# Another sequence for the first 310 steps of a hand-ordered long convolution with an MLP

## The chip, the cores and the metric

The kernel runs on one core of one Trainium2 chip. The metric is the device time of one execution in microseconds, the median over runs of the same program. Beside the times there is one profiled execution of the kernel before, with its own time; all durations in this document up to the result are from that execution.

## The reference

Sequence length S is 2048, width D is 512, and everything arrives in bfloat16. The model is a gated long convolution followed by a channel-mixing MLP block:

```
k_shift = sum over 4 taps of shifted k times shift_k        (per channel)
kv      = k_shift * v
y       = irfft(rfft(kv, 4096) * rfft(ssm_k, 4096))[:2048] + kv * ssm_D
h       = q + layernorm(q) * y
x       = layernorm(h)
a       = gelu(layernorm(x) @ w1), its four quarters shifted by -1, +1, -2, +2 rows, @ w2
x1      = x + a
out     = h + x1 + gelu(layernorm(x1) @ w3) @ w4            (w3: 512 x 1792, w4: 1792 x 512)
```

The Fourier transforms are over the sequence, one for each of the 512 channels.

## The kernel before, in words

The sequence is cut into halves s = 0 and 1, and each half into eight blocks b of 128 rows. The transforms are done as matrix products in two steps with an exchange of data between partitions in the middle. Four signals are transformed: F0 and F1, the two halves of the filter, and A0 and A1, the two halves of kv. For each signal:

- S1 (L389): eight groups of products of the input blocks with the table f1 on TensorE, named by signal, b and hp.
- E1 (L257, a copy helper): ScalarE or VectorE copies two PSUM banks at a time to SBUF (1024 columns).
- X (L405): eight transfers SBUF to SBUF that regroup the data, named by signal, g and kl. X (sig, g, kl) needs all the E1 of b = 2g and 2g + 1. "X A0 (1,1)" in the title of the change is the one with g = 1 and kl = 1.
- S2 (L413): four groups of products with the table ftab, one for each kl; S2 for kl needs X (0, kl) and X (1, kl).
- E2: copies of the spectrum to SBUF (L257), or for F1 a sum on VectorE (L425).

Before A0 and A1 come the taps: K (L442) makes shifted k by products with diagonals dg, which are built from the taps on VectorE (L307) or POOL (L299), and KV (L450) on VectorE multiplies by v. Each K needs its k load and diagonal, and each KV the load of its half of v. The row with ssm_D is added to row 0 of the filter ("dr", L294, on POOL), which lets the kv * ssm_D term ride in the convolution; S1 of F0 for b = 0 needs it.

The tables are sines, made early: "ftv" computes integer phases (L341), "fta" takes them modulo 4096 (L343), "ft" is the sine on ScalarE (L344); "ttv", "tta" and "tts" make another table, "f2v", "f2a" and "f2s" a third. Then "glu" (L367) loads the Gelu table on ScalarE, after which A0's E1 follow.

The inverse has the spectrum products P (L474, VectorE), the products I2 (L484), their copies EV, eight transfers XI (L495) for each half, and I1 (L502). H (L616) adds q's part: z_t (step Y, L613 on POOL or VectorE, L611 on ScalarE) holds the normalised q, whose statistics Q (L506) run on VectorE as each q block arrives. Then come the two layer norms, w1 (L699), w2 (L722), w3 (L777) and w4 (L790) with the sum of L792 and a store.

Nothing of the order is left to a scheduler. Every piece of work is added to a plan under a number, with a function that issues it, and the string ORDER lists all 784 steps:

```
for word in ORDER.split():
    t, slots, i = self.t[int(word[:3])], [int(c) for c in word[4:]], 0
    ...
        t["fn"](word[3], t["got"].get("ps", slots))
```

The first three digits of a word are the number of the step, the letter is the engine that does it (S SyncE, P TensorE, V VectorE, A ScalarE, G POOL), and the digits behind are the buffers it takes: PSUM banks, or slots of a pool. Each engine does its own steps in the order of the string; across engines they wait for each other by semaphores. A word that changes its letter moves the work to another engine.

All loads, exchanges and stores are issued by SyncE in the order of its words and use one queue. In the built program they take turns on eight semaphores, so each transfer waits until the eighth before it has landed. A load step is no more than this:

```
def load(name, dst, src, deps=(), size=0):
    add(name, {SP: ...}, lambda e, s: nc.sync.dma_start(dst, src), deps, size=size)
```

Names of loads: Lf (half, b) are filter blocks of 256 KB, Lk (half, c) blocks of k of 260 KB, Lv (half, g) parts of v of 512 KB, Lq (half, g) blocks of q of 256 KB, Lw1 to Lw4 the weights. ftab, the integer phases and the A0 spectrum share memory, as do several other pairs, so some orders are fixed by reuse.

Of the kernel before, what the change touches and what calls it, by code (L numbers as in the profile page):

```python
# [33 lines left out]
052A 015S 049G 094V 073S 097P0 054A 040V 024S 050G 091P1 090V 068S 041A 096V 099P4 070S 092V 048A 072S 100V 107P23 069S 103P67 098V 017S 108A 109P45  # L34
067S 111P01 110V 104A 018S 115P23 116A 105P67 323V 113P45 324V 112A 211P20 106V 114A 117P01 212V 119S 084P6745 118A 326V 071S 085A 086V 081P2301 123S
120S 082A 215P6 329V 020S 327V 083A 078P4523 124S 330V 217P7 125S 080A 216V 121S 079A 075P0123 218V 122S 325V 126S 076A 127P6745 328V 011S 128A 219P01
129V 016S 331G 012S 077A 013S 220V 130P6745 139V01 132A 133P2301 131A 141V23 134A 140P45670 147V45 142P 135A 149V67 143A 148P23011 155V01 150P 144A
145S 221P4 152A 146S 157V23 014S 151A 136P6701 222V 138A 137V 153S 156P23452 319G 158P 154S 332G 163V45 225P0 159A 223P1 165V67 160A 161S 164P67230
162S 226V 166P 224V 175P45 167A 168V 333G 213P0 176A 337G0 169S 183P67 170S 340G1 343V2 185P23 184A 214V 177P45 316S 334G3 186V 187P01 178A 189P67
188V 179P45 190A 181P23 180V 028S 182A 171P67 192S 172P01 196S 338V 173P23 191S 335V 339A 349G0 315S 344V 231P45 336A 346G3 195S 235P67 341V 232A  # L40
355G2 198S 347V 174P10 352G1 026S 236A 350V 194S 237P45 358G 356V 348A 193S 202P6723 345A 353V 197S 359G 342A 203V 239P01 238A 371G 360V 241P67 240A
204V 227P45 242A 372G 229P01 228V 230A 199P2367 247S 364G0 373V 233P45 351A 361G1 200V 234A 374G2 362P00 365P1 384V 354A 377G3 208P2345 244S 363V 366A
243S 201V 385G 375P01 367P1 318S 376A 246S 357A 386V 378P0 369P6 390V1 245S 379A 209V 397G 387A0 250S 382P7 248S 368A 210V 388P02 398G 391P2 249S
380P3 389A 025S 392V 370A 399G 263V01 317S 251P0145 383A 381A 393P2 252A 265V23 395P3 253A 027S 205P6701 400V2 396A 403V3 401P43 394A 267V45 404P5
502P3 405A 206V 402A 506P2 406P5 503V 408P4 507V 504A 269V67 508A 264P67231 407A 266P 558V 409A 268P 207V 270P 559G 498P5 560G 271A 272V 561G0 510P4
564G1 499V 494P0 274S 511V 562P10 565P6 495V 514P7 563A 275V01 566A 254P2345 567P60 277V23 256A 577P0 496A 255V 568A 569P1 578A 279V45 573P6 500A 515V
615G 257P4523 574A 575P0 281V67 570A 259A 571P1 501V 576A 579P7 509V 572A 413V 616G 276P23012 580A 517V 278P 513V 280P 282P 412V 617G 581P6 621G2
287V01 283A 258A 285S 505V 273S 512V 618A3 284A 516V 619P71 260P2345 582V 587G 622P0 262A 261V 584P1 583S 588G 623A 620V 289V23 414V 589G 624P00
291V45 636P6 625A 590G0 416V 634P7 293V67 288P45230 635A 411V 290P 592S 591A1 299V01 292P 637A 593S 294P 286S 301V23 628P0 630P7 303V45 629A 295A
632P6 305V67 631A 626P0 297S 633A 417V 296A 300P45671 410V 302P 627A 298S 415V 304P 306P 418V 641P0 307A 419G 308A 309S 310S 420G 430G3 421A0 638P2  # L50
642V 427A2 424G1 497V 643S 594S2 585V 320V 311P34 639V 312P56 640S 422V 313P70 425V 423A 433G0 428V 314P12 426A 436G1 431V 429A 595P30 445V 439A2
442G3 603P6 434V 432A 446G 605P4 437V 604A 447V 435A 597P5 458V 451G3 596A 607P0 438A 448V2 459G 598A 599P3 470V 471G 449P53 452P7 600A 601P6 450V
453A 460V 472G 440V 608A 454P3 602A 473G0 443V 461A1 456P5 441V 474G2 475S 606A 612P2 463S 444A 476S 462A3 482V 455A 464S 483G 457A 477S0 609P3 484V
485V0 486G1 321V 487S 488S 465S1 522P7 489S2 518P6 480P0 519V 478P1 523V 481A 520A 466P0 524A 468P4 479A 644V 467A 490P5 521V 645G 525V 492P6 491A
646V 469A 610V 534P7 493A 647V2 542P3 648V3 649S 535V 554P1 650S 536A 543V 546P0 537V 544A 322V 538P3 545V 651S3 555V 526P5 539V 556A 530P4 611S 547V
540A 586S 550P3 527V 672G 529V 528A 652P50 531V 654P6 551V 673G 653A 656P7 532V 674V 658P3 553V 676A0 675V1 660P1 657A 552V 677S 659A 678S 662P0 756V
661A 557V 655A 664P7 548A 549V 663A 679S0 533V 665A 666P3 700V 757G 613V 758G 728V 701G 669P2 702V 703V2 704G3 705S 614S 729G 706S 730G 760G1 680P40
670V 707S1 686P5 759V0 681A 731V2 667V 688P4 762S 732V3 541V 682P1 761S 668S 684P0 733S 734S 692P6 685A 763S2 689A 708P70 693A 712P0 687A 735S3 714P6
713A 710P0 720P2 711A 764P30 721A 715A 772P0 709A 716P2 736P40 742P5 737A 717A 748P4 683A 738P2 776P1 774P6 777A 743A 766P7 749A 746P1 775A 768P6 747A
770P1 769A 767A 740P5 773A 744P4 765A 741A 771A 778P3 739A 745A 690P2 779V 780S 691A 694P6 750P7 695V 696S 671S 697P6 718P0 719A 725P5 722P4 726V 698V  # L60
727S 699S 753P5 723V 751V 724S 752S 781P4 754V 755S 782V 783S
"""


# [779 lines left out]
```

## Time and profile before

| what | value |
|---|---|
| median of 3 runs | 214.98 us |
| lowest and highest of them | 213.88 and 215.58 us |
| time of the profiled execution | 213.75 us |
| its span, first to last instruction | 211.8 us |
| busy: TensorE | 197.2 us, 93% of the span |
| busy: VectorE | 143.6 us, 68% |
| busy: ScalarE | 127.4 us, 60% |
| busy: POOL | 70.3 us, 33% |
| mean granted TensorE clock | 0.992 |
| share of the chain that ended last on TensorE | 67% |
| on ScalarE, DMA, VectorE, SyncE's queue | 9%, 9%, 7%, 3% |
| moved by the one DMA queue | 32.55 MB |

The profile's page gives busy times over the whole span, which hides that the stages differ: the transforms of the first half and most loads lie in the first third, the MLP in the rest. The views by stretches and the timeline are therefore of more use here than the sums. "Idle before" in brackets in a timeline row is the time that the engine stood still ahead of that row, with what ended it. SPq rows are the issue of a transfer, not its duration; a transfer lands later.

### The profile page before, as it was taken

How to read it: one execution, taken by the hardware profiler on the slowest of the kernel's cores; microseconds unless marked ns; L12 is line 12 of the kernel's file. 1: busy time of each engine (PE TensorE's matmuls, PEld its weight loads, DVE VectorE, ACT ScalarE, POOL GpSimd, SP SyncE). 2: the span in 40 equal slices, each digit the busy share in tenths (PEclk: the TensorE clock that was granted, in tenths of full speed). 3: DMA queues.
4: the chain of work that ended last, by engine and by line, in shares of the span. 5: the costliest groups of instructions: out<-in, count | busy, mean ns of one | idle time of the engine just before them, and what ended most of it. 6: DMA issues, size and time to landing. Idle time of an engine off the chain costs nothing.

```text
span 211.8 us, 5064 instructions
## 1 busy us (share of the span) xinstructions
PE 197.2 (93%) x1980; PEld 117.8 (56%) x1980; DVE 143.6 (68%) x312; ACT 127.4 (60%) x211; POOL 70.3 (33%) x160
## 2 busy tenths in 40 slices
PE   7978876899788999999999999999999999999992
PEld 5544332343237556746654784665848888645440
DVE  6759988999999999999986973389945000020231
ACT  3769996977998965863582984365711655610100
POOL 7480039900995531623007783022370000000000
PEclk9999997999999999999999999999999999999999
DMA  6999698488878994032236007823246600001021
GB/s 179 316 395 384 223 325 321 122 234 257 299 291 286 329 437 144 3 84 68 75 101 176 26 4 178 120 50 99 51 116 156 128 0 0 3 25 50 25 74 50
DMA packets 30808, 32.85 MB, mean 155 GB/s; under 512 B 20545, under 2 KB 22594, under 8 KB 30530
## 3 DMA queue, kind: packets, MB, share of 16 engines
q1 hardware_dynamic: 30786, 32.55, 50.0%
q8 instruction: 15, 0.25, 0.5%
q14 instruction: 7, 0.06, 0.1%
HBM read 13.14 MB, written 4.46 MB: 83 GB/s over the span
## 4 chain that ended last, share of the span: by engine, by line
PE 67%; ACT 9%; DMA 9%; DVE 7%; SPq 3%; issue 3%; ACTq 0%; DVEq 0%
PE ps L777 22%; PE ps L790 20%; PE ps L699 7%; PE ps L722 6%; PE ps L484 5%; ACT r_a L257 4%; DMA r_v<-in_v_dram 4%; DMA r_a<-r_a 3%; SPq L266 2%; ACT r_vs L257 2%; DVE r_p L474 2%; PE ps L502 2%; DMA r_z<-r_vs 2%; PE ps L389 1%; PE ps L413 1%
## 5 line engine op out<-in xcount | busy, mean ns | idle before, releaser
L777 PEld LDWEIGHTS <-r_k 128*128 128x128 bf16 x448 | 43.6, 98 | 7.5 <-issue 0.8
L792 DVE TENSOR_TENSOR r_v<-ps,r_v 128x512 bf16<-128x512 f32 x16 | 10.8, 687 | 46.6 <-PE ps L790 46.6
L474 DVE TENSOR_TENSOR r_p<-r_a,r_f 128x2048 bf16<-128x2048 bf16 x24 | 29.1, 1246 | 0.6 <-ACT r_a L257 0.4
L777 PE MATMUL ps<-r_dg,r_k 128*128 128x256 bf16 x224 | 25.8, 273 | 0.0
L257 ACT CAST r_a<-ps 128x1024 bf16<-128x1024 f32 x23 | 22.4, 1028 | 3.3 <-PE ps L413 2.9
L613 POOL TENSOR_SCALAR z_t<-r_q,qrs,qnm 128x512 f32<-128x512 bf16 x12 | 13.2, 1108 | 13.0 <-DVE r_v L616 12.3
L781 ACT ACTIVATE r_a<-ps 128x512 bf16<-128x512 f32 x14 | 7.9, 609 | 13.8 <-PE ps L777 13.8
L257 ACT CAST r_vs<-ps 128x1024 bf16<-128x1024 f32 x14 | 13.7, 1019 | 4.1 <-PE ps L484 4.1
L257 ACT CAST r_f<-ps 128x1024 bf16<-128x1024 f32 x14 | 13.4, 1031 | 4.5 <-PE ps L389 4.5
L442 PE MATMUL ps<-r_dg,r_k 128*128 128x256 bf16 (+3 forms) x112 | 15.5, 289 | 0.6 <-ACT r_f L257 0.6
L781 ACT ACTIVATE r_f<-ps 128x512 bf16<-128x512 f32 x14 | 7.8, 606 | 13.6 <-PE ps L777 13.6
L484 PE MATMUL ps<-r_p,ttab 32*64 32x512 bf16 x384 | 14.1, 409 | 0.9 <-ACT r_a L257 0.3
L725 DVE SCALAR_TENSOR_TENSOR r_q<-r_v,hrr,ps 128x512 bf16<-128x512 bf16 x16 | 11.3, 743 | 4.9 <-PE ps L722 4.9
L389 PEld LDWEIGHTS <-f 128*32 128x32 bf16 x256 | 7.1, 101 | 12.8 <-issue 8.3
L442 PEld LDWEIGHTS <-r_k 128*128 128x128 bf16 x112 | 9.4, 98 | 8.5 <-issue 4.3
L699 PEld LDWEIGHTS <-r_fx 128*128 128x128 bf16 x128 | 12.2, 98 | 2.5 <-issue 0.4
L777 PE MATMUL ps<-xtx,r_k 128*128 128x256 bf16 x112 | 13.0, 273 | 0.0
L777 PE MATMUL ps<-xty,r_k 128*128 128x256 bf16 x112 | 12.9, 273 | 0.0
L450 DVE TENSOR_TENSOR r_kv<-ps,r_v 128x512 bf16<-128x512 f32 x16 | 10.4, 682 | 3.5 <-DMA r_v<-in_v_dram 3.4
L790 PE MATMUL ps<-w4s,r_f 128*128 128x512 bf16 x56 | 12.7, 379 | 0.0
L748 POOL TENSOR_TENSOR xrr<-xrr,mhalf 128x2 f32<-128x2 f32 x8 | 6.8, 850 | 17.6 <-DVE xrr L745 17.3
L790 PE MATMUL ps<-w4s,r_v 128*128 128x512 bf16 x56 | 12.6, 380 | 0.0
(181 smaller groups left out, 364.7 us busy)
## 6 DMA issues: line engine op xcount, KB each, us to landing
r_z<-r_vs SPq DMA_DIRECT2D x16, 256.0 KB, 3.6
r_k<-in_kt_dram SPq DMA_DIRECT2D x8, 260.0 KB, 4.9
r_v<-in_v_dram SPq DMA_DIRECT2D x4, 512.0 KB, 7.5
r_q<-in_q_dram SPq DMA_DIRECT2D x8, 256.0 KB, 8.0
r_f<-r_f SPq DMA_DIRECT2D x8, 256.0 KB, 4.8
r_a<-r_a SPq DMA_DIRECT2D x8, 256.0 KB, 4.9
r_f<-r_a SPq DMA_DIRECT2D x8, 256.0 KB, 4.4
r_a<-r_z SPq DMA_DIRECT2D x8, 256.0 KB, 8.4
```

The source lines that it names most:

```text
L257: (act.copy if e in "AM" else on[e].tensor_copy)(o, i)
L442: nc.tensor.matmul(o[:, (d + j0) * P:(d + j1 + 1) * P], lhsT=kT[s][c][:, bb, x:x + P], rhs=diag[:, c, j0:j1 + 1, :].rearrange("p j x -> p ...
L474: on[e].tensor_tensor(out=prs[:, sl[0]:sl[0] + 2, :, :], in0=sp[a][:, kl, :, :, :], in1=gv, op=MUL)
L484: nc.tensor.matmul(ps[64 * t:64 * t + 64, bk[h], :], lhsT=ttab[32 * h:32 * h + 32, 2 * kl + t, 2 if x else xx, :], rhs=prs[32 * h:32 * h + ...
L613: on[e].tensor_scalar(out=z_t[:, sl[0], :], in0=qs, scalar1=qrs[:, i:i + 1], scalar2=qnm[:, i:i + 1], op0=MUL, op1=ADD)
L699: nc.tensor.matmul(ps[:, sl[0], j * 256:(j + 1) * 256], lhsT=w1s[:, k, m * P:(m + 1) * P], rhs=xt[:, k, :], start=(k == 0), stop=(k == DC ...
L722: nc.tensor.matmul(ps[:, sl[0], :], lhsT=h1T[s][:, m, bb, x:x + P], rhs=w2s[:, m, :], start=(m == 0), stop=(m == DC - 1))
L725: vec.scalar_tensor_tensor(out=q_sb[:, s, b, :], in0=h_sb[s][:, b, :], scalar=hrr[:, 4 * s + b // 2, 0, b % 2:b % 2 + 1], in1=ps[:, got((" ...
L777: nc.tensor.matmul(ps[:, sl[0], j * 256:(j + 1) * 256], lhsT=w3s[:, k, fc * P:(fc + 1) * P], rhs=xt[:, k, :], start=(k == 0), stop=(k == D ...
L781: act.activation(gb[:, 2 * fp:2 * fp + 2, :], ps[:, got(("M", s, p, fp))[0], :].rearrange("p (j x) -> p j x", j=2), ACT.Gelu_apprx_tanh)
L790: nc.tensor.matmul(ps[:, sl[0], :], lhsT=gb[:, fc, (b % 2) * P:(b % 2 + 1) * P], rhs=w4s[:, fc, :], start=(fc == 0), stop=(fc == FC - 1))
L792: add(("Z", s, b), {V: 0.61}, lambda e, sl, b=b: vec.tensor_tensor(out=h_sb[s][:, b, :], in0=ps[:, got(("O", s, b))[0], :], in1=h_sb[s][:, ...
```

## The change

Only the string ORDER changes. Words 1 to 310 or so (up to place 339, with small swaps near the end) stand in another sequence; from there to the end all words keep their sequence and engine, and only the numbers of PSUM banks and pool slots are renamed. The first lines of the diff:

```
-004S 029P0 000S 002S 003S 005S 008S 031V 037V 009S 030P 063P23 006S 055P45 001S 057P67 064V 007S 056A 038G 065P01 010S 023S 058A 059P45 045G 019S
-061P23 033V 066A 021S 087P60 039V 095P71 036G 046V 101P0 042V 047A 060A 034G 093P1 032G 062A 043V 051P45 074S 088V 035G 044A 053P23 022S 102V 089P6
...
+004S 029P0 000S 002S 003S 005S 008S 031V 037V 001S 030P 063P23 006S 055P45 009S 057P67 064V 007S 056A 038G 065P01 010S 019S 058A 059P45 045G 033V
+061P23 060A 087P60 036V 039G 062A 095P71 046V 042V 066A 093P4 032G 047A 074S 101P5 043V 015S 034G 022S 044A 051P23 094V 023S 053P01 088V 052A 035G
...
```

By names, engine by engine (the order before, then the new one):

- SyncE, first loads: Lk(0,0) Lk(0,3) Lv(0,0) Lk(0,1) Lf(0,0) Lk(0,2) Lv(0,1) Lq(0,2) Lv(1,0) Lq(0,0) X F0 (1,3) ... becomes Lk(0,0) Lk(0,3) Lf(0,0) Lk(0,1) Lv(0,0) Lk(0,2) Lv(0,1) Lv(1,0) X F0 (1,3) Lk(1,0) Lq(0,1) Lq(0,2) X F0 (1,1) Lq(0,3) Lq(0,0) ...
- SyncE, the A0 exchange: X A0 (0,0), X F0 (1,0), X A0 (1,0), (0,1), Lv(1,1), X A0 (1,1), (1,2), (0,2), (0,3), (1,3), Lf(1,0), Lk(1,1), Lf(1,1) becomes X F0 (1,0), X A0 (0,0), (1,0), (0,1), (1,1), Lv(1,1), X A0 (1,2), (0,2), Lf(1,1), Lf(1,0), Lk(1,1), X A0 (0,3), (1,3).
- SyncE, later: Lw1 and Lw2 change places; Lq(1,1) goes from among the F1 exchanges to behind X A1 (1,3); X A1 (0,3) and (0,2) go ahead of Lw3.
- VectorE and POOL: ftv goes from VectorE to POOL, the diagonal for c = 3 from POOL to VectorE, a small memset (edge0, L573) from POOL to VectorE, and Y (0,3), one z_t, from VectorE to POOL. POOL does dr ahead of the diagonal for c = 1, not behind it.
- VectorE: the gating products KV run in the order (0,3), (0,0), then fta, (0,1), (1,0), (0,2), (1,3), (1,1), (1,2). Before: (0,0), (1,3), (0,3), fta, (0,1), (1,0), (0,2), (1,2), (1,1). Two E1 of F1 change places between VectorE and ScalarE.
- ScalarE: E1 F0 (2,0) and (2,1) go ahead of f2s and of E1 F0 (3,1); some copies of the same kind and three HS (L600) change places.
- TensorE: neighbours change places (K (0,3) and (1,3), K (0,2) and (1,1), five pairs of S1, one I1 and an S1).

More of the change, by code (lines that the diff above doesn't have):

```diff
@@ L36 @@
[L36 to L59, printed above, removed]
@@ new lines @@
+150P 144A 145S 221P4 333G 157V23 152A 146S 337G0 014S 151A 136P0123 222V 343G1 137V 138A 156P45672 153S 340G2 158P 154S 334G3 163V45 225P2 159A 223P3
+160A 165V67 161S 164P01450 162S 226V 166P 224V 175P67 167A 168V 213P2 176A 169S 183P01 214V 170S 185P45 184A 187P67 315S 186V 177P23 188A 189P01 178V
+179P45 190A 181P67 180V 171P01 028S 182A 172P23 338V 192S 231P67 196S 335V 339A 349G0 173P45 316S 344V 336A 346G3 193S 341V 235P01 232A 355G1 195S
+347V 174P32 236A 352G2 191S 350V 237P67 198S 358G 342A 356V 202P0145 197S 348A 353V 194S 345A 359G 204V 239P23 238A 371G 203V 241P45 240A 227P67 242A
@@ new lines @@
+229P23 372G 360V 228V 230A 199P0145 247S 361G0 373V 233P67 351A 364G1 200V 362P20 234A 374G2 365P3 384V 366A 377G3 208P0167 245S 363V 354A 375P31 243S
+201V 385G 367P2 376A 244S 357A 378P3 386V 246S 369P4 379A 390V0 318S 209V 397G 387A1 382P5 248S 370A 250S 388P32 210V 368A 398G 391P4 026S 380P0 389A
+249S 383A 392V 399G 251P2367 263V01 025S 381A 393P1 317S 252A 265V23 027S 395P0 253A 205P4523 396A 400V2 394A 403V3 401P03 267V45 404P1 502P6 405A
+206V 402A 506P7 406P1 503V 408P0 507V 504A 269V67 508A 264P45671 407A 266P 558V 409A 268P 207V 270P 559G 498P1 560G 271A 272V 561G1 510P0 564G0 499V
@@ new lines @@
+494P2 274S 511V 562P30 565P4 495V 514P5 563A 275V01 566A 254P6701 567P40 277V23 256A 577P2 496A 255V 568A 569P3 578A 279V45 573P4 500A 515V 615G
+257P0167 574A 575P2 281V67 570A 259A 571P3 501V 576A 579P5 509V 572A 413V 616G 276P67232 580A 517V 278P 513V 280P 282P 412V 617G 581P4 621G2 287V01
+283A 258A 285S 505V 273S 512V 618A3 284A 516V 619P51 260P6701 582V 587G 622P2 262A 261V 584P3 583S 588G 623A 620V 289V23 414V 589G 624P20 291V45 636P4
+625A 590G1 416V 634P5 293V67 288P01670 635A 411V 290P 592S 591A0 299V01 292P 637A 593S 294P 286S 301V23 628P2 630P5 303V45 629A 295A 632P4 305V67 631A
@@ L62 @@
+731V2 667V 688P0 762S 732V3 541V 682P3 761S 668S 684P2 733S 734S 692P4 685A 763S2 689A 708P50 693A 712P2 687A 735S3 714P4 713A 710P2 720P6 711A 764P70
+721A 715A 772P2 709A 716P6 736P00 742P1 737A 717A 748P0 683A 738P6 776P3 774P4 777A 743A 766P5 749A 746P3 775A 768P4 747A 770P3 769A 767A 740P1 773A
+744P0 765A 741A 771A 778P7 739A 745A 690P6 779V 780S 691A 694P4 750P5 695V 696S 671S 697P4 718P2 719A 725P1 722P0 726V 698V 727S 699S 753P1 723V 751V
+724S 752S 781P0 754V 755S 782V 783S
 """
```

16 lines of the change are left out of this document (12 added, 4 removed).

## The prediction

> **What bounds the kernel now.** I read the page first, then the chain of work that ended last, the busy time by stretches, and the timeline of the first 50 us, where every moved step lies.
>
> ```profile
> span 211.8 us, 5064 instructions
> PE   7978876899788999999999999999999999999992
> DVE  6759988999999999999986973389945000020231
> ...
> ```
>
> Each digit is the busy share of a fortieth of the span (5.3 us) in tenths. TensorE has no gap worth naming from its fourteenth slice (about 69 us) until the end; its loose slices are the first thirteen, where the change lies. VectorE is just as full from its fourth slice to its twentieth.
>
> ```profile
> 10.00:15.00 5.00, 3.83 (x40) 2.23 (x38) 2.79 (x5) 3.40 (x5) 3.77 (x7) 1.00 1.06 416
> 25.00:30.00 5.00, 4.39 (x63) 1.95 (x63) 4.88 (x9) 5.00 (x7) 0.21 (x2) 1.00 0.79 255
> 30.00:35.00 5.00, 2.48 (x41) 0.90 (x40) 3.78 (x4) 3.15 (x4) 4.70 (x11) 0.97 1.00 365
> 35.00:40.00 5.00, 4.68 (x75) 2.00 (x73) 4.63 (x5) 4.76 (x6) 4.81 (x4) 0.69 0.36 128
> 100.00:110.00 10.00, 9.77 (x177) 6.42 (x175) 9.97 (x14) 6.81 (x12) 0.00 (x0) 1.00 0.34 86
> ```
>
> The columns are the stretch, then busy time of PE, weight loads, VectorE, ScalarE and POOL, the granted clock, the DMA share and GB/s. From 30 to 35 us PE works half the time and VectorE three quarters; this is the only slack stretch between 15 us and the end in which both wait. From 100 to 110 us both are full. So whatever the first 45 us save moves the rest forward as a block; whatever they save ahead of a full engine that gets no less work is handed back.
>
> ```profile
> 5.61 8.06 DMA r_v<-in_v_dram
> 13.79 1.29 DVE r_kv L450 x2
> 15.08 0.98 DVE r_a L343
> 16.09 1.15 ACT ftab L344
> 17.26 1.28 ACT L367
> 18.66 2.05 ACT r_a L257 x3
> 24.15 1.03 ACT r_f L257
> 26.56 0.59 SPq L266
> 27.20 5.42 DMA r_a<-r_a
> 32.75 0.67 PE ps L413 x16
> ...
> 35.42 1.99 PE ps L484 x26
> ```
>
> The chain (start, length, what) says it in order: the second half of v lands at 13.67 us, VectorE gates with it, the sine table and the Gelu table follow on ScalarE, which then evacuates from 18.66 us on; SyncE issues the second half of v for the second half-sequence at 26.56 us and only then X A0 (1,1), which lands at 32.62 us, and the second transform of A0 starts at 32.75 us.
>
> **The change part by part.** Part one, the start.
>
> ```profile
> 7.81 1.32 DVE L341 TENSOR_SCALAR r_a<-r_a,sv 128x512 int32<-128x512 int32 x2
> 7.98 0.87 POOL L299 TENSOR_SCALAR_AFFINE_SELECT r_dg<-r_k 128x512 bf16<-128x512 bf16 x1 [1.27 <-DMA r_k<-in_kt_dram]
> 7.16 0.74 DVE L307 TENSOR_SCALAR r_dg<-ident,r_k 128x128 bf16<-128x128 bf16 x4 [1.12 <-DMA r_k<-in_kt_dram]
> 9.53 1.90 ACT L257 CAST r_f<-ps 128x1024 bf16<-128x1024 f32 x2
> 11.12 0.63 POOL L299 TENSOR_SCALAR_AFFINE_SELECT r_dg<-r_k 128x512 bf16<-128x512 bf16 x1 [2.27 <-DMA r_k<-in_kt_dram]
> 11.80 1.14 POOL L294 TENSOR_TENSOR r_fx<-r_fx,r_vs 1x512 bf16<-1x512 bf16 x1
> 12.99 1.05 PE L389 MATMUL ps<-r_fx,f 128*32 128x512 bf16 x16 [1.17 <-POOL r_fx L294]
> 13.79 1.29 DVE L450 TENSOR_TENSOR r_kv<-ps,r_v 128x512 bf16<-128x512 f32 x2 [2.17 <-DMA r_v<-in_v_dram]
> ```
>
> PE waits 1.17 us for the row sum of filter block 0 (L294), which POOL does behind a diagonal (L299) that itself waits 2.27 us for k. In the new order L294 stands ahead of that diagonal and block 0 is loaded two places earlier, ahead of the first half of v and of k block 1. Three transfers change places among themselves, so the last of them still ends near 11.7 us (the diagonal's k landed at 11.1 us, and L294 found block 0 there 0.7 us later): block 0 then lands near 8.7 us and the first half of v near 11.7 us instead of 10.3. POOL has first the two table operations that VectorE did in 1.32 us; on POOL I bound them by 1.3 us and by 4.2 us (two at 2.1 us, a row on z_t below), so L294 ends between 9.9 and 12.1 us. PE reaches its matmuls at 11.82 us: 0.9 to 1.17 us of its wait goes. VectorE takes one diagonal more (0.74 us) while it waited anyway.
>
> The gating is reordered: before, the second product needs the second half of v, and VectorE sat 2.17 us; now four that need only the first half stand in front. From 11.75 us: two products at 0.65 us, the table's AND (L343, 0.98 us on the chain), then six more products end at 18.2 us instead of 19.0. The AND ends at 14.2 us instead of 16.06, and from its end to ScalarE's first A0 evacuation the chain has 2.6 us (18.66 less 16.06), so that could start at 16.8 us. PE, some 1.1 us ahead of before, ends the first A0 product at 17.1 us. ScalarE begins the A0 evacuations at 17.2 us, not 18.66: 1.45 us gained there.
>
> Part two, from there to the exchange; the rows are of the timeline, SPq being the issue queue, and the last one is from the instructions on r_v.
>
> ```profile
> 20.58 1.28 DVE L506 BATCH_NORM_STATS2 qst<-r_q 128x6 f32<-128x512 bf16 x2
> 23.05 0.52 SPq L405 DMA_DIRECT2D r_a<-r_a  x1
> 24.31 2.21 SPq L405 DMA_DIRECT2D r_a<-r_a  x2
> 27.20 3.64 SPq L405 DMA_DIRECT2D r_a<-r_a  x5
> 29.63 1.23 DVE L257 CAST r_a<-ps 128x1024 bf16<-128x1024 f32 x1
> 32.07 0.69 DVE L450 TENSOR_TENSOR r_kv<-ps,r_v 128x512 bf16<-128x512 f32 x1 [1.22 <-DMA r_v<-in_v_dram]
> 32.68 2.35 DVE L474 TENSOR_TENSOR r_p<-r_a,r_f 128x2048 bf16<-128x2048 bf16 x2
> 35.40 5.05 DVE L474 TENSOR_TENSOR r_p<-r_a,r_f 128x2048 bf16<-128x2048 bf16 x4 [0.37 <-ACT r_a L257]
> 35.48 6.36 POOL L613 TENSOR_SCALAR z_t<-r_q,qrs,qnm 128x512 f32<-128x512 bf16 x3
> 46.97 0.54 DVE L613 TENSOR_SCALAR z_t<-r_q,qrs,qnm 128x512 f32<-128x512 bf16 x1
> DMA to landing us min/median/max: 5.4/7.5/8.6
> ```
>
> All of q's first half now queues behind v's first 512 KB of the other half-sequence and behind four other transfers: after the 13.67 us of v's second half stand nine units of 256 KB before the q block that VectorE's statistics need first; at 416 GB/s that is 0.63 us each, so it lands at 19.4 us, 20.5 if an issue stalls (every transfer here waits for the eighth before it). VectorE arrives at 19.4 us. I take 0.35 us of waiting. Behind that statistics row on VectorE stand the A0 evacuation and, behind it, SyncE's first A0 exchange: 22.45 us instead of 23.05. VectorE then does the same list to the cast that began at 29.63 us, plus the edge memset: it now begins near 29.15 us. So of 1.45 us about 0.5 is left: VectorE has hardly a gap in this stretch (4.88 of 5 us between 25 and 30).
>
> Part three, the exchange. Before, SyncE spends 0.6 us on an F0 exchange between the first and second A0 one, then 2.21 us on the next two, then v, then X A0 (1,1) at 27.20 us. Now the F0 one is already gone (it waits only for older transfers) and the order is A0, A0, A0, X A0 (1,1), v. At 0.6 us an issue, with ScalarE's sixth A0 evacuation ready at 23.1 us (17.2 us and the 5.5 us that six took from 18.66 to 24.15, and 0.4 us for a k product of PE in between), (1,1) is issued at 24.3 us and v at 24.9 us; if one issue takes the extra 1.0 us seen at 24.31 us, at 25.3 and 25.9. As many transfers stand ahead of v as before, so 5.4 us from issue to landing (the row's smallest, and that of this transfer, since VectorE got it at 32.0 us) gives 30.3 to 31.3 us; I take 30.9. The transform then waits for VectorE's cast (30.4 us) instead of for (1,1): 2.3 us earlier than 32.75, but it isn't last. Last is v, since VectorE has the k-v product (L450) in front of the spectrum products (L474). L450 ends at 31.6 us and L474 begins then instead of at 32.68: 1.1 us. The 0.37 us wait in the next row goes too, since its casts start 2 us earlier. The sum on VectorE at 40 us: 1.1 + 0.37 = 1.47 us, bounds 0.9 (v at 31.4) and 1.85 (v under VectorE's own 30.3).
>
> Part four, one z_t (0.54 us at 46.97 us) goes from VectorE to POOL. The next cast behind it starts as PE's matmul ends, so nothing is gained there; cover gone, it would be 0.54. POOL's row shows 2.1 us each, so four end near 44 us instead of three near 42; their reader (L616) is further back on VectorE than the z_t at 46.97 us. A rule of the Trainium skill speaks against it: "SBUF — State Buffer", section "SBUF: two separate sides", has VectorE operations with two SBUF inputs and GpSimd operations that read SBUF exclude each other for a whole instruction. By the rows the four products beside z_t took 1.26 us each against 1.18 in the pair before, 0.08 more. By the rule one more z_t could cost VectorE up to its whole own time, and the gain would be less by that.
>
> The weight loads of w1 and w2 change places, a q block goes from before the F1 exchanges to behind the A1 ones, and w3 goes behind two A1 exchanges: all still ahead of their use.
>
> ```profile
> r_k<-in_w_dram SPq DMA_DIRECT2D x1, 1792.0 KB, 9.0
> 82.53 3.39 PEld L777 LDWEIGHTS <-r_k 128*128 128x128 bf16 x32 [0.41 <-DMA r_q<-in_q_dram]
> ```
>
> w3 takes 9.0 us to land and is first read at 82.53 us; SyncE has its issue behind two exchanges more, 1.2 us, and its place in the sequence is still some ten microseconds ahead of that, so 0; without that cover it would be 1.2 us. The last 445 steps keep their order and engines; only bank numbers differ.
>
> The sum: 1.47 us, rounded 1.5. The profiled execution took 213.75 us, 1.95 above its span of 211.8, so 212.25 for one like it; the median shown is 214.98, 1.23 us higher, so I forecast 213.5 us.
>
> **The rivals.**
>
> First, more: with the early transform the gap of PE between 30 and 35 us may go under what drops its clock (0.97 and 0.69 in the two rows; at half speed that is 0.3 and 3.1 us, 3.4 in all). The 1.99 us of L484 on the chain then take 1.0 us, v lands before 30.3 us, and z_t's 0.54 counts: 1.85 us from there, 0.4 us of L484's 1.0 that lies on the chain ahead of VectorE's next product, and 0.54: 2.8 us, 212.2 us. Against it: PE still waits between the products at 1.2 us each. The Trainium skill ("TensorE: Matmul & The Clock Gate", "Part 1: The HAM clock gate") has a free-running window of about 3.4 us that decides on the clock; the trace's half-speed spell fits it, and by that the drop may merely fall somewhere else.
>
> Second, nothing: VectorE's full stretch hands back all. If q lands at 20.5 us, its 0.5 us goes; if v lands at 31.9 us, only the 0.37 us is left, which the next exchange wait can take: 214.7 to 215.0 us. For it: VectorE's 4.88 of 5. In this case the change does what it says (block 0 and (1,1) come earlier) and neither was last.
>
> Third, slower: v, now behind one A0 exchange more in its own queue, lands late, and L450 holds every L474 behind it. The row for r_v goes up to 8.6 us from issue to landing: 24.9 + 8.6 = 33.5 us, L474 begins at 34.2 us instead of 32.68, and with the 0.37 us spared the loss is 1.2 us: 216.2 us. It decides from a landing of 32.4 us on. For it: the same queue also has three new loads behind v, ahead of two exchanges. Against it: the loads that took 8.6 us had the queue full before them; at 25 us the share is 0.79.
>
> **How the numbers follow.** Forecast 0.45, more 0.22, nothing 0.15, slower 0.18. The forecast's own range is 212.9 to 214.3 us (0.9 to 1.85 us, with 0.2 about it). The runs of before spread from 213.9 to 215.6 us, so I let the range reach over the first rival and nearly all of the third: 211.7 to 216.2 us. One per cent, 2.15 us, is about what a measurement of this kernel can tell from no change. Faster by more than that: the first rival and a quarter of the forecast's scatter, 0.34. Slower by more than that needs the third with scatter on top: 0.12. Within: 0.54.
>
> **What would show it.** In the changed profile: PE's matmuls of filter block 0 without the 1.17 us wait; the Gelu table load near 15.6 us; the first A0 exchange at 22.5 us; (1,1) issued before 25.5 us; the first L474 at 31 to 32 us without a wait of 0.37 us behind it; the steady stretch of PE beginning 1.5 us earlier. Wrong if L450 waits for r_v past 32 us, if the statistics wait for r_q more than 1 us, or if L474 begins 1.5 us earlier and the end does not follow.

## The result

| | before | changed |
|---|---|---|
| median, lowest and highest of 20 runs each | 214.24 us, 212.09 to 215.58 | 212.9 us, 211.56 to 214.98 |
| ratio of changed to before | | 0.9931, 95% interval 0.9905 to 0.9957 |
| profiled execution, and its span | 213.75 us, 211.8 | 211.95 us, 209.8 |
| mean granted TensorE clock in it | 0.992 | 1.000 |

The ratio is 1.5 us of 214.24, with an interval from 0.9 to 2.0 us. A second session gave 0.9954 (0.9920 to 0.9988), 1.0 us. The ratios and intervals leave out executions more than 1.5% above the fastest of their kernel: two of the changed kernel's twenty here, up to nine of 35 of the kernel before in the sessions below.

The page of the changed kernel, the same three lines as before:

```profile
span 209.8 us, 5064 instructions
PE   7999775999889999999999999999999999999992
DVE  6997989999999999999968862489935000020231
```

The loose slices are still in the first quarter, the rest is the same wall of nines. By stretches (start and end, busy PE, weight loads, VectorE, ScalarE, POOL, granted clock, DMA share, GB/s):

```profile
10.00:15.00 5.00, 4.94 (x49) 2.96 (x48) 4.93 (x9) 3.85 (x6) 3.10 (x6) 1.00 1.00 382
30.00:35.00 5.00, 2.41 (x64) 0.65 (x59) 4.08 (x5) 4.62 (x6) 4.67 (x6) 1.00 0.96 362
35.00:40.00 5.00, 3.93 (x87) 1.76 (x87) 5.00 (x6) 4.49 (x5) 4.89 (x4) 1.00 0.56 159
```

PE now works 4.94 of the 5 us from 10 to 15 us (3.83 before) and VectorE 4.93 (2.79). From 30 to 35 us PE still works only half the time. From 35 to 40 us the clock is full where it had been 0.69, and PE's work there takes 3.93 us instead of 4.68. The chain of work that ended last, its pieces up to 32 us:

```profile
2.49 3.62 DMA r_k<-in_kt_dram
6.13 3.33 DVE r_dg L307 x8
...
14.36 1.05 ACT ftab L344
15.43 1.28 ACT L367
...
24.17 1.35 SPq L405
...
27.41 3.65 DMA r_q<-in_fx_dram
...
31.53 1.23 DVE r_p L474
```

v's second half no longer opens the chain; the first k block and eight diagonals on VectorE do. The sine table is at 14.36 us instead of 16.09. X A0 (1,1) is issued at 24.17 us, 27.2 before. Just ahead of L474 the chain goes through a filter block issued behind v, which landed at 31.06 us, within 0.3 us of v: two waits end almost together there. The timeline of the same execution:

```profile
8.26 1.14 POOL L294 TENSOR_TENSOR r_fx<-r_fx,r_vs 1x512 bf16<-1x512 bf16 x1
11.44 1.05 PE L389 MATMUL ps<-r_fx,f 128*32 128x512 bf16 x16
16.83 5.57 ACT L257 CAST r_a<-ps 128x1024 bf16<-128x1024 f32 x6
19.84 1.28 DVE L506 BATCH_NORM_STATS2 qst<-r_q 128x6 f32<-128x512 bf16 x2 [1.32 <-DMA r_q<-in_q_dram]
22.31 3.21 SPq L405 DMA_DIRECT2D r_a<-r_a  x4
25.57 0.59 SPq L266 DMA_DIRECT2D r_v<-in_v_dram  x1
28.68 1.21 DVE L257 CAST r_a<-ps 128x1024 bf16<-128x1024 f32 x1
29.76 0.79 PE L413 MATMUL ps<-r_a,ftab 64*32 64x512 bf16 x16
30.92 0.69 DVE L450 TENSOR_TENSOR r_kv<-ps,r_v 128x512 bf16<-128x512 f32 x1 [1.04 <-DMA r_v<-in_v_dram]
31.53 6.90 DVE L474 TENSOR_TENSOR r_p<-r_a,r_f 128x2048 bf16<-128x2048 bf16 x6
```

Block 0's products (PE L389) stand without a wait; the second A0 transform starts at 29.76 us, 32.75 before; v is still what L450 waits for, and all six L474 run without the 0.37 us wait between them.

### The profile page after: what moved, and what is told of

It is laid out like the page before. It is cut to its first block, busy times and chain, and to the rows that moved or that the text cites. A ratio compares the mean times of both kernels' runs of the same rounds, so it can differ in the third digit from the quotient of the medians.

```text
span 209.8 us, 5064 instructions
## 1 busy us (share of the span) xinstructions
PE 196.0 (93%) x1980; PEld 116.6 (56%) x1980; DVE 143.8 (69%) x314; ACT 127.6 (61%) x211; POOL 72.2 (34%) x161
## 4 chain that ended last, share of the span: by engine, by line
PE 64%; DVE 14%; ACT 8%; DMA 6%; SPq 3%; issue 3%; POOL 0%; DVEq 0%; ACTq 0%
PE ps L777 23%; PE ps L790 20%; PE ps L722 6%; PE ps L699 4%; PE ps L484 4%; DVE r_p L474 3%; ACT r_a L257 3%; DMA r_dg<-dhb 2%; DVE r_v L616 2%; PE ps L502 2%; SPq L405 2%; DVE r_f L425 2%; DMA r_q<-in_fx_dram 2%; DMA r_k<-in_kt_dram 2%; DVE r_dg L307 2%
## 5 line engine op out<-in xcount | busy, mean ns | idle before, releaser
L474 DVE TENSOR_TENSOR r_p<-r_a,r_f 128x2048 bf16<-128x2048 bf16 x24 | 28.5, 1225 | 0.2
L613 POOL TENSOR_SCALAR z_t<-r_q,qrs,qnm 128x512 f32<-128x512 bf16 x13 | 15.3, 1186 | 9.9 <-DVE r_v L616 9.2
L442 PE MATMUL ps<-r_dg,r_k 128*128 128x256 bf16 (+3 forms) x112 | 15.5, 288 | 0.9 <-ACT r_f L257 0.8
L484 PE MATMUL ps<-r_p,ttab 32*64 32x512 bf16 x384 | 12.6, 379 | 2.1 <-DVE r_p L474 1.5
L442 PEld LDWEIGHTS <-r_k 128*128 128x128 bf16 x112 | 9.5, 98 | 9.0 <-issue 4.2
L699 PEld LDWEIGHTS <-r_fx 128*128 128x128 bf16 x128 | 12.3, 98 | 3.1 <-issue 0.8
L389 PEld LDWEIGHTS <-f 128*32 128x32 bf16 x256 | 6.2, 96 | 11.9 <-issue 8.2
L790 PE MATMUL ps<-w4s,r_f 128*128 128x512 bf16 x56 | 12.7, 379 | 0.0
L790 PE MATMUL ps<-w4s,r_kv 128*128 128x512 bf16 x56 | 12.4, 379 | 0.0
```

The costliest lines, as they stand in the source:

```text
L442: nc.tensor.matmul(o[:, (d + j0) * P:(d + j1 + 1) * P], lhsT=kT[s][c][:, bb, x:x + P], rhs=diag[:, c, j0:j1 + 1, :].rearrange("p j x -> p ...
L474: on[e].tensor_tensor(out=prs[:, sl[0]:sl[0] + 2, :, :], in0=sp[a][:, kl, :, :, :], in1=gv, op=MUL)
L484: nc.tensor.matmul(ps[64 * t:64 * t + 64, bk[h], :], lhsT=ttab[32 * h:32 * h + 32, 2 * kl + t, 2 if x else xx, :], rhs=prs[32 * h:32 * h + ...
L613: on[e].tensor_scalar(out=z_t[:, sl[0], :], in0=qs, scalar1=qrs[:, i:i + 1], scalar2=qnm[:, i:i + 1], op0=MUL, op1=ADD)
L699: nc.tensor.matmul(ps[:, sl[0], j * 256:(j + 1) * 256], lhsT=w1s[:, k, m * P:(m + 1) * P], rhs=xt[:, k, :], start=(k == 0), stop=(k == DC ...
L790: nc.tensor.matmul(ps[:, sl[0], :], lhsT=gb[:, fc, (b % 2) * P:(b % 2 + 1) * P], rhs=w4s[:, fc, :], start=(fc == 0), stop=(fc == FC - 1))
```

## The experiments

All but the last move one or more words of ORDER, or change the engine of one; the last is the changed kernel as it is. In the first eight kernels the string takes two lines less, so in their rows L448 is L450, L472 is L474, L440 is L442, L387 is L389, L411 is L413, L403 is L405, L292 is L294, L297 is L299 and L504 is L506. The first four ran on one chip, the next four on a second, the last four on a third, each group with runs of the kernel before beside it; a ratio is always to those.

**Filter block 0 ahead of v, alone.**

```
-037V 009S 030P 063P23 006S 055P45 001S 057P67
+037V 001S 009S 030P 063P23 006S 055P45 057P67
```

> The kernel before with one load moved: filter block 0 ahead of the first half of v, nothing else. Theory (only what reaches the first L474 on VectorE counts, and the gating of A0 waits for v's second half): PE's 1.17 us wait on L294 goes or shrinks under 0.5 us, but the AND (L343) still ends at 16.1 us because the second product in VectorE's order needs the second half of v at 13.7 us. ScalarE begins A0's evacuations at 18.4 to 18.7 us, L474 begins at 32.4 to 32.8 us, time within 0.3 us of before. Rival (the named edit gains by itself): PE runs 1.1 us earlier and the end follows, 1.0 to 1.2 us faster than before.

Measured: ratio 0.9992 (0.9960 to 1.0024). The theory on the time held, its reason did not. From the timeline:

```profile
11.05 0.64 POOL L297 TENSOR_SCALAR_AFFINE_SELECT r_dg<-r_k 128x512 bf16<-128x512 bf16 x1 [2.76 <-DMA r_k<-in_kt_dram]
11.65 1.14 POOL L292 TENSOR_TENSOR r_fx<-r_fx,r_vs 1x512 bf16<-1x512 bf16 x1
12.84 1.05 PE L387 MATMUL ps<-r_fx,f 128*32 128x512 bf16 x16 [1.36 <-POOL r_fx L292]
```

PE's wait did not go, it grew from 1.17 to 1.36 us. The row sum stands behind a diagonal on POOL that waits 2.76 us for k, and no earlier load of block 0 moves that.

**The gating order, alone.**

```
-053P23 022S 102V 089P6 ... 054A 040V 024S
+053P23 022S 089P6 ... 054A 040V 102V 024S
```

> The kernel before with one word of VectorE moved: the gating product (1,3), the one that needs v's second half, behind the AND (L343); all loads as before. Theory: the AND ends near 13.3 us instead of 16.06, but PE's wait on L294 is still there, so ScalarE reaches the sine only after its F0 evacuations, near 15.6 us: A0's evacuations begin at 18.2 to 18.5 us instead of 18.66, time 0 to 0.5 us faster than before. Rival (the gating order was the whole gain at the start): A0's evacuations begin at 17.2 us or earlier, time 0.8 us faster or more.

Measured: 1.0013 (0.9974 to 1.0051), no gain; A0's evacuations began at 19.02 us, later than both theories said.

```profile
15.82 3.68 DVE L448 TENSOR_TENSOR r_kv<-ps,r_v 128x512 bf16<-128x512 f32 x6 [1.25 <-PE ps L440]
```

VectorE no longer waits for v but for the k products of PE, which stand behind block 0's.

**Both of these.**

> The kernel before with both: filter block 0 loaded ahead of v's first half and the gating product (1,3) behind the AND; q, v's other half and the exchange in the order of before. Theory: each gate hid the other, so together ScalarE begins A0's evacuations 1.0 to 1.45 us earlier (17.2 to 17.7 us), more than the two single edits added; VectorE is full from there and X A0 (1,1) still behind v, so 0.3 to 0.9 us faster than before. Rival 1: all of the 1.45 us arrives at the end. Rival 2: VectorE hands all back, within 0.2 us of before.

Measured: 1.0032 (0.9998 to 1.0067), rather slower; A0's evacuations at 19.36 us. The theory fell: the two together don't open the gate. The same wait is 1.85 us here:

```profile
16.16 3.08 DVE L448 TENSOR_TENSOR r_kv<-ps,r_v 128x512 bf16<-128x512 f32 x5 [1.85 <-PE ps L440]
```

A third piece was missing, which these kernels left as it was: the row sum's place on POOL.

**X A0 (1,1) ahead of v, alone.**

```
-020S 327V 083A 078P4523 124S 330V
+124S 020S 327V 083A 078P4523 330V
```

> The kernel before with one transfer moved on SyncE: X A0 (1,1) issued ahead of the second 512 KB of v. Theory: the transform of A0 that needs (1,1) begins near 30 to 31 us instead of 32.75, but v is issued about 0.6 us later, so L450 and the first L474 begin 0 to 0.6 us later; the 0.37 us wait among the products goes. Time within 0.4 us of before, either way. Rival (the exchange was the limit, as the title has it): L474 at 40 us is 1 to 2 us earlier and the time 1 to 2 us shorter.

Measured: 0.9984 (0.9951 to 1.0017), as the theory said; L474 began 0.2 us later than before, behind a wait of 1.49 us for v, and its 0.37 us wait was gone.

**The changed kernel with v back ahead of X A0 (1,1).**

```
-124S 083A 215P6 020S
+020S 124S 083A 215P6
```

> The changed kernel with one transfer put back on SyncE: the second 512 KB of v issued ahead of X A0 (1,1), all else as changed. Theory: v is issued 0.6 to 1.3 us earlier and L450 with it, so the first L474 begins 0.3 to 1.0 us earlier than 31.53 us, but the transform that waits for (1,1) is 1 to 2 us later and its products with it; within 0.6 us of the changed kernel. Rival (the exchange's place is the gain): the time goes back by 1 us or more towards before.

Measured: 1.0042 (1.0005 to 1.0079): the whole gain is gone, as the rival had it. Alone the exchange was worth 0.2%, in the changed order about 1%. The two figures compare sessions on different chips. The profiled execution shows a part of why:

```profile
21.39 1.29 DVE L504 BATCH_NORM_STATS2 qst<-r_q 128x6 f32<-128x512 bf16 x2 [1.79 <-DMA r_q<-in_q_dram]
28.34 1.36 PE L440 MATMUL ps<-r_dg,r_k 128*128 128x512 bf16 x7
33.28 6.91 DVE L472 TENSOR_TENSOR r_p<-r_a,r_f 128x2048 bf16<-128x2048 bf16 x6
```

The first L474 comes at 33.28 us, not earlier but later. v didn't hold it: VectorE waited 1.79 us for q, and further on 1.24 us for a group of seven k products of PE, which took 1.36 us (1.03 elsewhere) at a granted clock of 0.66 from 25 to 30 us. The six L472 run without the 0.37 us wait here too, although (1,1) is behind v. How much of the 2 us is the exchange's place and how much the clock of this execution stays open. The loss in time is not a matter of the clock alone: the four executions without a stretch of lower clock are 0.58 us slower than such executions of the kernel before.

**The changed kernel with the q block that is read first in front of the other q blocks.**

```
-022S 044A 051P23 ... 091P6 021S 049G
+021S 022S 044A 051P23 ... 091P6 049G
```

> The changed kernel with one load moved: the block of q that VectorE's statistics (L506) read first goes ahead of the other three. Theory: the 1.32 us wait at 19.8 us is a real loss; without it VectorE's A0 evacuation starts near 20 us and the first A0 exchange is issued at 21.0 to 21.4 us instead of 22.31, v up to 1 us earlier, L474 near 30.6 us; 0.5 to 1.0 us faster than the changed kernel. Rival (v's landing is set by the queue and not by its issue, or VectorE waits for PE instead): the wait moves to another row and the time is within 0.3 us.

Measured: 1.0007 (0.9973 to 1.0041): not faster than the changed kernel, rather 0.5 to 0.8% slower.

```profile
21.77 3.23 SPq L403 DMA_DIRECT2D r_a<-r_a  x4
31.12 0.69 DVE L448 TENSOR_TENSOR r_kv<-ps,r_v 128x512 bf16<-128x512 f32 x1 [1.37 <-DMA r_v<-in_v_dram]
```

The wait for q went, the first A0 exchange was issued 0.54 us earlier and v at 25.04 instead of 25.57 us, and yet v landed at 31.1 us. That fits the rival, that the landing is set by what the queue still has to move more than by the issue; one profile doesn't show it. Ten of its twelve executions had a stretch of lower clock (below); why this order has it so often isn't shown.

**The changed kernel with v ahead of the first A0 exchange.**

```
-119S 326V ... 215P6 020S
+020S 119S 326V ... 215P6
```

> The changed kernel with one load moved: the second 512 KB of v goes ahead of the first A0 exchange. Theory (v's landing is the last wait ahead of L474): v is issued near 20 to 22 us and lands by 28 us, the 1.04 us wait of L450 goes, L474 begins at 30.5 to 30.9 us; 0.5 to 1.0 us faster than the changed kernel. Rival (the exchanges behind it in the queue pay): A0's exchanges land 0.6 to 1.3 us later, the transform takes over as the last wait, and the time is the same or up to 0.7 us slower.

Measured: 0.9918 (0.9884 to 0.9952), 212.08 us median, the lowest of all kernels. Its interval overlaps both of the changed kernel's, so it beats before, and is not shown to beat the changed one.

```profile
21.14 0.60 SPq L264 DMA_DIRECT2D r_v<-in_v_dram  x1
29.02 0.63 PE L411 MATMUL ps<-r_a,ftab 64*32 64x512 bf16 x16 [1.34 <-DMA r_a<-r_a]
29.80 1.23 DVE L255 CAST r_a<-ps 128x1024 bf16<-128x1024 f32 x1 [0.94 <-ACT r_f L255]
31.54 6.90 DVE L472 TENSOR_TENSOR r_p<-r_a,r_f 128x2048 bf16<-128x2048 bf16 x6
```

Theory and rival are both in the trace: v no longer holds L450, and the A0 exchange, now behind v, holds the transform for 1.34 us instead.

**The changed kernel with both, q and v.**

> The changed kernel with both moves: the first q block that the statistics read goes ahead of the others, and v's second 512 KB goes ahead of the first A0 exchange. Theory: the two waits lie one behind the other on VectorE, so both gains add: L474 near 30 us, 1.0 to 1.8 us faster than the changed kernel. Rival (something else, PE's transform or its S1 of F1, is next in line): no more than the better of the two single moves, under 0.8 us.

Measured: 0.9959 (0.9921 to 0.9998), the rival: L474 at 31.55 us, as with v alone, though the first A0 exchange was issued 0.4 us earlier. The transform's wait for the exchange was 1.34 us again.

**The kernel before with the start of the changed one: load, row sum ahead of the diagonal on POOL, gating order.**

```
-009S ... 001S      -034G 093P1 032G      -102V ... 040V
+001S 009S ...      +032G 034G 093P1      +... 040V 102V
```

> The kernel before with the three moves of the start: filter block 0 loaded ahead of v's first half, the row sum (L294) on POOL ahead of the diagonal that waits for k, and the gating product (1,3) behind the AND. All loads of q and v's other half and the exchange as before. Theory (the row sum's place on POOL, not the load, was what PE waited for): PE's wait on L294 goes, the gating no longer waits 1.85 us for PE, ScalarE begins A0's evacuations at 17.2 to 17.8 us instead of 18.66 and L474 follows by 0 to 0.6 us; v and X A0 (1,1) keep their order, so the time is 0.2 to 0.7 us shorter than before. Rival 1 (the start was the whole gain): 1.2 us shorter or more. Rival 2 (with X A0 (1,1) behind v nothing arrives at the end): within 0.2 us.

Measured: 0.9965 (0.9935 to 0.9996), 0.75 us, nearest to the theory. Against the kernel with load and gating alone the one more word, 032G, is worth 0.7% (by ratios from two chips).

```profile
8.42 1.30 POOL L294 TENSOR_TENSOR r_fx<-r_fx,r_vs 1x512 bf16<-1x512 bf16 x1
8.64 1.14 DVE L365 TENSOR_SCALAR r_a<-r_a 128x64 int32<-128x64 int32 x1
11.46 1.18 PE L389 MATMUL ps<-r_fx,f 128*32 128x512 bf16 x16
31.76 2.35 DVE L474 TENSOR_TENSOR r_p<-r_a,r_f 128x2048 bf16<-128x2048 bf16 x2
34.48 5.05 DVE L474 TENSOR_TENSOR r_p<-r_a,r_f 128x2048 bf16<-128x2048 bf16 x4 [0.37 <-ACT r_a L257]
```

PE's wait is gone, the gating still waits 0.67 us for PE, and L474 is 0.92 us earlier with its 0.37 us wait still there. The row sum's move without the other two was not run; it may carry all of this.

**The same with X A0 (1,1) ahead of v.**

```
-020S 327V 083A 078P4523 124S 330V
+124S 020S 327V 083A 078P4523 330V
```

> The kernel before with the three moves of the start and X A0 (1,1) issued ahead of v's second 512 KB; the loads of q, k and the weights, z_t, the diagonals and the tables' engines as before. Theory (start and exchange together are the change, everything else in it is filler): L474 begins at 31.3 to 31.9 us, the time is 1.0 to 1.7 us shorter than before, the same as the changed kernel within 0.4 us. Rival (the q blocks behind v and the other small moves carry part of it): less than half of the changed kernel's gain, under 0.7 us.

Measured: 0.9936 (0.9901 to 0.9970), 1.4 us. These four words bring what the changed kernel brings, within what can be measured; the other moved words are not shown to bring anything. Some of them may cost: the changed kernel with v back ahead of (1,1) has the start too, and yet it was 0.8% slower than the start alone. The q blocks behind v, for which VectorE waited 1.79 us there, are one candidate, but the kernel in which that wait went by another order of q was not faster either; it stays open. The exchange's own part here, 0.3%, lies inside both intervals, and in the profiles L474 begins later with it (32.08 us, the theory had 31.3 to 31.9) than without (31.76). In the timeline the 0.37 us wait is gone:

```profile
32.08 6.90 DVE L474 TENSOR_TENSOR r_p<-r_a,r_f 128x2048 bf16<-128x2048 bf16 x6
```

**The changed kernel with v ahead of the first A0 exchange and ftv back on VectorE.**

```
-036V 039G 062A      -119S 326V ... 215P6 020S
+036V 039V 062A      +020S 119S 326V ... 215P6
```

> The changed kernel with v's second 512 KB ahead of the first A0 exchange and the two table operations ftv (L341) back on VectorE. Theory (VectorE and POOL hinder each other at 6 to 10 us: eight diagonals took 3.3 to 3.6 us beside ftv on POOL, where four took 0.74 alone): diagonals and ftv on VectorE take about 2.8 us together, the AND ends 0.4 to 0.8 us earlier and ScalarE's A0 evacuations with it; but q's first block and the exchange stay where they are, so 0 to 0.5 us faster than with v's move alone, the best time of all kernels near 211.7 us. Rival (POOL needs the port too or VectorE waits for v's first half at 11.7 us): the gain is under 0.1 us, or the loss up to 0.5 us.

Measured: 0.9958 (0.9923 to 0.9992), not better than v's move alone.

```profile
6.15 0.81 DVE L307 TENSOR_SCALAR r_dg<-ident,r_k 128x128 bf16<-128x128 bf16 x4
7.14 0.74 DVE L307 TENSOR_SCALAR r_dg<-ident,r_k 128x128 bf16<-128x128 bf16 x4 [0.18 <-DMA r_k<-in_kt_dram]
7.80 1.83 DVE L341 TENSOR_SCALAR r_a<-r_a,sv 128x512 int32<-128x512 int32 x2
7.91 1.44 POOL L294 TENSOR_TENSOR r_fx<-r_fx,r_vs 1x512 bf16<-1x512 bf16 x1 [1.15 <-DMA r_fx<-in_fx_dram]
29.79 0.62 PE L413 MATMUL ps<-r_a,ftab 64*32 64x512 bf16 x16 [2.22 <-DMA r_a<-r_a]
```

Eight diagonals took 1.55 us instead of 2.84 to 3.61, but L341 now met the row sum and took 1.83 us (1.32 before). The evacuations of A0 began at 17.32 us, 0.3 earlier than with v's move alone; then the exchange landed later still (2.22 us of waiting) and took it all back.

**The changed kernel, profiled once more.**

> The changed kernel itself, profiled a second time. Theory (of the 2.0 us between the two profiled spans about 1 us is the luck of that execution, in which the first k block landed so early that VectorE began its diagonals at 6.13 us without a wait, where every other kernel waited 0.9 to 1.3 us): this time the diagonals begin at 6.9 to 7.3 us, ScalarE's A0 evacuations at 17.6 to 17.9 us and L474 at 31.8 to 32.5 us; the time stays 0.5 to 0.9 per cent under before. Rival (the early k belongs to the change's order of loads): the diagonals begin again at 6.1 to 6.3 us.

Measured: 0.9954 (0.9920 to 0.9988), and a span of 212.0 us where the first profiled execution had 209.8, both at a clock of 0.998 or more.

```profile
span 212.0 us, 5064 instructions
...
5.48 4.46 PE L389 MATMUL ps<-r_fx,f 128*32 128x512 bf16 x40 [0.90 <-DMA r_fx<-in_fx_dram]
6.81 3.61 DVE L307 TENSOR_SCALAR r_dg<-ident,r_k 128x128 bf16<-128x128 bf16 x8 [0.76 <-DMA r_k<-in_kt_dram]
13.46 1.05 PE L389 MATMUL ps<-r_fx,f 128*32 128x512 bf16 x16
18.70 1.93 ACT L257 CAST r_a<-ps 128x1024 bf16<-128x1024 f32 x2
21.78 1.29 DVE L506 BATCH_NORM_STATS2 qst<-r_q 128x6 f32<-128x512 bf16 x2 [1.43 <-DMA r_q<-in_q_dram]
33.26 0.69 DVE L450 TENSOR_TENSOR r_kv<-ps,r_v 128x512 bf16<-128x512 f32 x1 [1.43 <-DMA r_v<-in_v_dram]
33.87 6.90 DVE L474 TENSOR_TENSOR r_p<-r_a,r_f 128x2048 bf16<-128x2048 bf16 x6
```

The rival's early k did not come back here; it did in the kernel with ftv back on VectorE (6.15 us), so two of the seven profiles with this order of loads have it and none of the other seven. Luck fits this best; a part of the order in it isn't excluded. The sizes were missed: ScalarE's A0 evacuations at 18.70 us where 17.6 to 17.9 was expected, L474 at 33.87 where 31.8 to 32.5 was. Another filter block came so late that PE waited 0.90 us at the beginning, and block 0's products stood 2.0 us later than in the first execution. This execution was the slowest of its twelve (214.15 us), the first one the third fastest of its twenty (211.95), so the two profiles show the ends of the scatter and not its middle.

**The three stretches.** From the same timelines: the start of ScalarE's first A0 evacuation; from there to the first L474; from there to the pair of L474 behind the A0 cast that began at 41.03 us in the kernel before; and from that pair to the end. All in us.

| kernel | to A0's evacuation | to first L474 | to the pair | to the end | half-speed clock |
|---|---|---|---|---|---|
| before | 18.66 | 14.02 | 9.68 | 169.4 | 3.4 |
| load alone | 18.07 | 14.62 | 10.32 | 169.7 | 6.8 |
| gating alone | 19.02 | 13.47 | 9.68 | 169.3 | 3.4 |
| load, gating, no row sum | 19.36 | 13.59 | 10.47 | 169.2 | 6.8 |
| exchange alone | 18.59 | 14.29 | 10.00 | 169.3 | 6.8 |
| start alone | 17.77 | 13.99 | 9.68 | 169.3 | 3.4 |
| start and exchange | 18.08 | 14.00 | 10.00 | 169.2 | 6.8 |
| changed, first profile | 16.83 | 14.70 | 8.74 | 169.5 | 0 |
| changed, second profile | 18.70 | 15.17 | 8.74 | 169.4 | 0.8 |
| changed, v back | 17.94 | 15.34 | 8.79 | 169.6 | 3.4, ahead of L474 |
| changed, q first | 17.58 | 14.15 | 10.01 | 169.7 | 6.8 |
| changed, v early | 17.66 | 13.88 | 9.08 | 169.9 | 3.4 |
| changed, q and v | 17.80 | 13.75 | 8.79 | 170.3 | 0, 1.3 near the end |
| changed, v early, ftv back | 17.32 | 14.98 | 9.18 | 169.5 | 0, 1.3 near the end |

The half-speed time is worked out from the mean clock: 0.992 of 211.8 us lacks 1.7 us of full speed, which at half speed is 3.4 us. Read down the columns: the last but one lies between 169.2 and 169.7 us but for two kernels with v early (169.9 and 170.3, of which the second lost clock near the end), so little after 43 us takes part. The first gains some 0.9 us in the changed order (17.58 to 17.94 us in the four kernels that share it, 16.83 and 18.70 in the two profiles of the change itself). The second is 0.7 and 1.15 us longer in the two profiles of the change, which wait 1.32 and 1.43 us for q. The third, at 6.8 us of half speed, is 10.32 and 10.47 us with (1,1) behind v and 10.00 to 10.01 with it ahead, so the early (1,1) gains 0.3 to 0.5 us there; each 3.4 us of half speed that doesn't occur in it gains 0.3 to 0.9 us more. In the changed order it is as short with v back ahead of (1,1) (8.79) as without (8.74): there L474 begins late enough that (1,1) no longer holds it.

## Why the prediction was right, step by step

The forecast was 1.5 us less; measured were 1.5 (0.9 to 2.0) and 1.0 us (0.3 to 1.7). The time itself, 213.5 us, was 0.6 us too high, because it started from the median of three runs (214.98 us; 214.24 over twenty).

*The start.* Right in mechanism: the row sum ahead of the diagonal was the piece that freed PE; without it neither the load nor the gating order nor both gained anything in time. (With it, load or gating order were not left out one at a time.) Too large in size: forecast were 1.45 us for ScalarE's A0 evacuations, about 0.9 came (0.7 to 1.1 in the four kernels that share this start; 1.8 and none in the two profiles of the change itself). The mis-sized term is VectorE's "one diagonal more (0.74 us) while it waited anyway": beside the table operations and the row sum on POOL eight diagonals took 2.84 to 3.61 us, not 1.48, and behind them VectorE had no wait to hide this in: it was ready for the gating at 12.3 to 12.7 us in those four kernels and the second profile, where 11.75 was forecast. The bound for ftv on POOL held (1.55 us, between 1.3 and 4.2).

*From there to the exchange.* The place was right, the size not: the wait for q was taken at 0.35 us and was 1.32 and 1.43 us, above the 1 us that the prediction itself named as a sign of being wrong. In the first profile the block landed at 19.8 us where 19.4 was forecast (the block is itself the ninth of the nine units that the prediction sets ahead of it); VectorE simply arrived at 18.5 us. In the second the block landed at 21.8 us, later than the 20.5 taken for a stall. So most of the start's gain was given back here, as the prediction had it ("of 1.45 us about 0.5 is left"), with both terms off: 0.9 gained, 0.7 and more returned. And the wait is not worth its length: without it v landed no earlier.

*The exchange.* (1,1) was issued at 24.17 us (24.3 forecast), v at 25.57 (24.9), L474 began at 31.53 (31.6). That so many rows agree to a tenth was luck: the execution began 1 us early by its first k block, which covered the 1 us more of waiting for q. The second profile has L474 at 33.87 us, of the same program. The 0.37 us wait did go, in every kernel with (1,1) ahead of v, and that the transform isn't last but v is was right. But the wait went as well with v ahead of (1,1) in the changed order, so the exchange's place is not the only way to it. In the second profile L450 waited for v until 33.26 us, past the 32 us that the prediction named as another sign of being wrong. The upper bound of the prediction's sum doesn't add up: v 0.6 us earlier than 30.9 us makes 2.07 us, not 1.85.

*z_t and the weights.* Nothing in the runs speaks against 0: the last column but one of the table doesn't move. But the 2.1 us each is a mean of unlike rows. In the first profile two z_t on POOL took 0.77 us each, and two beside the products on VectorE 3.72 and 2.78 us: the mutual exclusion that the prediction priced on VectorE, at 0.08 us, was paid by POOL.

*The rivals.* "More" was partly there. No stretch of lower clock (counted as a mean clock of 0.996 or more) occurs in 17 of 30 executions of the changed kernel and in 24 of 93 of the kernel before. At like clock the changed kernel is faster by 0.36 us (no drop, 212.55 against 212.91), 0.84 (3.4 us of it) and 0.46 (6.8 us); this pools sessions on different chips, and within the one session that has the clocks of both it is 0.50, 1.10 and 0.41 us, from 8, 2 and 2 executions of the changed kernel. With the shares of the changed kernel the executions of before would average 0.37 us less. So some 0.4 us of the gain came with the clock and the rest, some 0.5 us, from the order at like clock; for the first session this can't be worked out, since the clocks of before aren't on record there. The same working, on means, leaves 0.6 of 0.9 us for the start alone, 0.95 of 1.3 for start and exchange, 0.95 of 1.4 for v early, and only 0.1 of 0.65 for q and v. Why an order has the drop less often isn't shown. The prediction had it as a rival apart, with a gain of 2.8 us; it is a matter of odds, and part of the likeliest case, so the agreement of 1.5 with 1.5 us is in part luck. What it said against itself, that the drop may merely fall somewhere else, is seen in the kernel with v back ahead of (1,1), which had it at 25 to 29 us. "Nothing", at most 0.3 us, is excluded by the first interval (0.9 us and more); the second only touches it. "Slower" did not occur in the times. Its condition, a landing of v past 32.4 us, occurred in the second profile, but through a late issue (27.63 us): from issue to landing v took 5.2 us in the first profile and 5.5 us in the second, where 5.4 was taken and 8.6 feared.

## What to carry to other kernels

Ask what stands ahead of a late operation on its own engine before asking for its data earlier: moving the load, the gating order or both changed nothing, and one more word on POOL made the difference. Where several waits end at almost the same time, each move alone can be worth nothing while the set is worth the gain, so test the set, and then the set less one. And take two profiles of one program before believing a span: here they differed by 2.2 us, more than the change.

## What the runs showed of the hardware

The granted clock falls to half mostly for 3.4 or 6.8 us (mean clock 0.992 or 0.984), in some executions of a program and not in others. In these profiles the drop comes behind a stretch in which PE has gaps: before, PE worked 0.64 of the 3 us from 31 to 34 us, and the clock was 0.50 from 35 to 38 us; with v back ahead of (1,1) PE worked 2.5 of the 4 us from 22 to 26 us, and the clock was 0.50 from 26 to 29 us. The changed kernel has such a stretch too (2.41 and 2.67 of 5 us from 30 to 35 us) and no drop behind it in either profile. Medians of such a kernel move with the odds of it. This fits the free-running window of about 3.4 us in the Trainium skill ("TensorE: Matmul & The Clock Gate", "Part 1: The HAM clock gate"). That the window's phase decides which stretch is caught is an argument; no row shows the phase.

Some instructions of VectorE and POOL hold each other up for a whole instruction. In the kernel with the start alone, VectorE's L365, 0.18 us in most profiles, began at 8.64 us inside POOL's L294 and ended at 9.78 us, 0.06 us after it. Eight diagonals went from 1.55 us to 2.84 and more beside POOL's L341 and L294. Single rows of the changed kernel's first profile show both sides, a diagonal beside L294 (8.26 to 9.40 us), and z_t on POOL beside the products, which end at 38.43 us, and behind them:

```profile
8.25 1.21 DVE L307 TENSOR_SCALAR r_dg<-ident,r_k 128x128 bf16<-128x128 bf16 x1
35.19 3.72 POOL L613 TENSOR_SCALAR z_t<-r_q,qrs,qnm 128x512 f32<-128x512 bf16 x1
39.66 0.77 POOL L613 TENSOR_SCALAR z_t<-r_q,qrs,qnm 128x512 f32<-128x512 bf16 x1
```

Not every pair does it: four diagonals beside POOL's L363 took 0.81 us where four alone take 0.74. The Trainium skill ("SBUF — State Buffer", "SBUF: two separate sides") has this as an exclusive lock for the length of an instruction, for VectorE operations in a two-port mode or with two SBUF inputs, and the trace agrees in the rows named; the prediction weighed it only for z_t, where the product rows showed 0.08 us, and not for the start.

Loads at the very beginning come up to 1.25 us earlier or later from one profile to the next (first diagonals at 6.13 to 7.38 us over all kernels; 6.13 and 6.81 in the two of the changed kernel), and the stretches behind start from there.
